# Six blocks of 502 columns instead of eight of 376 in a Fourier transform followed by two MLPs

## The chip, the cores and the metric

One core of a Trainium2 chip runs the whole kernel. The metric is device time in microseconds, the median of several executions of the same program. The tables of cosines and sines are constants of the program, and the inputs lie in device memory when the clock starts.

## The reference

The input `x` has 2 batches of 3008 rows of 256 numbers. A Fourier transform over rows and columns is taken, of which the real part is kept, and every one of the 6016 rows of the result then goes through two MLPs of width 2048:

```python
X = np.fft.fft(x, axis=1)                 # x: 2 x 3008 x 256
X = np.fft.fft(X, axis=2).real
x = X.reshape(6016, 256)
h = x @ moe_w_in                          # 256 -> 2048
x = np.maximum(h, 0.0) ** 2 @ moe_w_out   # 2048 -> 256
h = x @ moe2_w_in
return (h - np.tanh(h)) @ moe2_w_out
```

## The kernel before

**Numbers in two parts.** Every operand of a TensorE product is split into a high part (12 bits) and a low rest, both stored as float32r, and a product is three matmuls: high by high, low by high, high by low (`products`, L350). ScalarE (ACT) makes the high part with a copy, VectorE (DVE) or GpSimd (POOL) the low part with a subtraction.

**The row transform as matmuls.** The rows of the spectrum come in pairs k and -k that share cosine and sine sums, so half of the spectrum is calculated, and each matmul column stands for a pair. There are four classes of k per batch (`KS`), of 378, 376, 376 and 376 columns. Classes 2 and 3 (odd k) come out of one pass, `dft_pair` (48 matmuls, in four PSUM banks); classes 0 and 1 (even k) each out of `dft_mm` (27 matmuls, three banks) on rows that were folded once more (`fold`, the steps from L320 on, then `split_even`). `fold` and `split_even` of the even rows run on POOL for batch 0. The column transform over 256 is multiplied into the first weights instead (`transform_in`).

**Blocks and steps.** A block is one class of one batch: eight blocks of 376 or 378 columns, in the order of `BLOCKS`. The first MLP runs over steps (block, f), f being one of 16 groups of 128 hidden units: `front` makes the hidden units of two halves (6 matmuls, into two of the rotating PSUM banks `w`), `mid` adds and squares them (3 DVE instructions, 3 ACT instructions), `late` makes the low part `gl` (2 POOL instructions), and `back` multiplies by the second weights and adds to four PSUM banks `a` (12 matmuls). `front` runs two steps ahead of `back`. The order of the steps is written out in `STEPS`: the first four f of block 0, all of block 1, the rest of block 0, then block by block.

**What is put beside the steps.** The weights of the first MLP are unpacked from 64-bit integers and transformed while the first steps run; `MADE` says in which step of the loop at L838 which f is made: `transform_in` (4 matmuls with 128 columns, which the profile shows as 8 records), `split_transformed_hi` and `_lo` (L251, L256), and a two-column copy over DMA (`middle_load`, tile `mcol`) after which POOL clears a row (`clear_middle`, L260) and stores two sums (`middle_add`, L274); only then may `front` read that f. The transform is written into the columns from 384 on of the same banks in which `front` put its 376 columns. Then come the folding of the even rows (`bg0`, `bg0s`), loading and folding batch 1 (`bg1`, `bg2`) and preparing the weights of the second MLP (`make_w2`, `bg3`, two pieces a step from step 48 on).

**The second MLP** goes over pairs of f with seven products instead of eight (`pair`, 21 matmuls into three of the `w` banks; `back_pair`, 24 matmuls into the banks `a`), on sums of weights (`sums`) that are loaded once and stay in SBUF for all blocks.

The engines' queues run in order; a scheduler of the tile framework, which sees the written order and the waits, fixes the order in each queue.

Of the kernel before, what the change touches and what calls it, by code (L numbers as in the profile page):

```python
# [9 lines left out]
F32 = mybir.dt.float32  # L10
# [34 lines left out]
BLOCKS = [(b, c) for b in range(B) for c in (2, 3, 0, 1)]  # L45
NBLK = len(BLOCKS)
OFF = np.concatenate([[0], np.cumsum([2 * NC[c] for _, c in BLOCKS])])
NTOT = int(OFF[-1])
# [75 lines left out]
def columns():  # L124
    idx = np.zeros(B * S, np.int64)
    for j, (b, c) in enumerate(BLOCKS):
        k = KS[c]
        for i, kk in enumerate(k):
            if c == 0 and i == NROW:
                continue  # L130
            p, m = int(kk) % S, int(-kk) % S
            if c >= 2 and kk % 4 == 3:
                p, m = m, p
            idx[b * S + p] = OFF[j] + i
            idx[b * S + m] = OFF[j] + NC[c] + i
    return idx


@with_exitstack
def spectral_mlps(  # L140
# [13 lines left out]
    NM = max(NC)  # L154
# [3 lines left out]
    wstack = ctx.enter_context(ExitStack())  # L158
    psw_pool = wstack.enter_context(tc.tile_pool(name="psw", bufs=2, space=PSUM))
# [4 lines left out]
    pools = {}  # L164

    def psw():

        if "w" in pools:
            return [pools["w"].tile([128, 512], F32, tag="w", name=f"w{m}", bufs=4) for m in range(2)]
        t = psw_pool.tile([128, 2, 512], F32, tag="w", name="w", bufs=2)  # L170
        return t

    def bank(p, m):
        return p[m] if isinstance(p, list) else p[:, m]
# [4 lines left out]
    def ring(name):  # L179

        return main.tile([128, 4, NM], F32R, tag="ring", name=name, bufs=8)

    def stage():
        return main.tile([128, 1024], F32, tag="stage", name="stage", bufs=4)
# [7 lines left out]
    wtab = main.tile([128, 2, 2, 128], F32, name="wtab")  # L192
# [48 lines left out]
    def transform_in(f, p):  # L241


        v = val[1, f]
        for m in range(2):
            for kt in range(2):
                cs = slice(kt * 128, (kt + 1) * 128)
                pe.matmul(p[:, m, 384:], wtab[:, kt, m, :], v[:, cs], start=(kt == 0), stop=(kt == 1))

    def split_transformed_hi(f, p):  # L250
        act.copy(wt[f][:, 0, :].rearrange("p (m f) -> p m f", m=2), p[:, :, 384:])  # L251

    def split_transformed_lo(f, p):
        hi = f32(wt[f][:, 0, :]).rearrange("p (m f) -> p m f", m=2)
        dst = wt[f][:, 1, :].rearrange("p (m f) -> p m f", m=2)
        dve.tensor_tensor(dst, p[:, :, 384:], hi, ALU.subtract)  # L256
# [21 lines left out]
    xp = {}  # L278

    def load_x(b, t):  # L280
        r = stage()
        sp.dma_start(r, x[b, t, 0])
        if b == 0:
            u = xp[t] = f32(ring("p")).rearrange("p a n -> p (a n)")[:, :1024]
            sp.dma_start(u, x[b, t, 1])
            for eng, cs in ((dve, slice(640)), (pool, slice(640, 1024))):
                eng.tensor_tensor(r[:, cs], r[:, cs], u[:, cs], ALU.add)
# [4 lines left out]
    def fold(b, t):  # L292

        r = xraw.pop((b, t))
        o = main.tile([128, 2, 4, 128], F32R, tag=f"xs{t}", name=f"xo{t}")
# [22 lines left out]
        e = main.tile([128, 4, 128], F32, tag=f"xf{t}", name=f"xf{t}")  # L318
# [14 lines left out]
    def split_even(b, t):  # L333

        e = main.tile([128, 2, 4, 128], F32R, tag=f"xs{t}", name=f"xe{t}")
# [644 lines left out]
```

## Time and profile before

| | |
|---|---|
| time, median of three executions | 992.44 us (990.68 to 993.64) |
| profiled execution: span from the first to the last instruction | 988.1 us |
| of it, TensorE matmul busy | 956.5 us (97%) |
| VectorE / ScalarE / GpSimd busy | 777.3 / 743.0 / 288.7 us |
| granted TensorE clock | 1.000 |

The page gives the profiled execution's own time as its span; the device time measured around the program adds what lies before the first and after the last instruction. Against the median the span is 4.3 us shorter. PE are matmuls and PEld the weight loads ahead of each of them; matmuls are pipelined, so that two overlap in a busy sum, and the pace is read from starts, not from the mean duration of one.

### The profile page before, as it was taken

The numbers are of one execution on the slowest core, as the hardware profiler recorded it, in microseconds if no ns is written. First come the engines' busy times: TensorE is split into PE (matmuls) and PEld (weight loads), VectorE is DVE, ScalarE is ACT, GpSimd is POOL, SyncE is SP. The second block draws the span as 40 slices with busy tenths as digits, with TensorE's granted clock in tenths as the row PEclk, the third lists the DMA queues.
The fourth block names the chain that finished last, engine by engine and source line by source line (L and its number), as shares of the span: only waits on it lengthen the run. The fifth ranks groups of instructions, "written<-read, shape, count | busy, mean of one in ns | idle before, by whom it ended". The sixth has DMA issues, their size and how long they took to land.

```text
span 988.1 us, 15509 instructions
## 1 busy us (share of the span) xinstructions
PE 956.5 (97%) x5530; PEld 944.8 (96%) x5530; DVE 777.3 (79%) x1444; ACT 743.0 (75%) x1319; POOL 288.7 (29%) x312
## 2 busy tenths in 40 slices
PE   4889999999999999999999999999999999999998
PEld 3778899999999999999899999999999999999998
DVE  5998567878988588888877878778787787877776
ACT  2988868888999789888866767667676676766665
POOL 2276717765676466766500000000000000000000
PEclk9999999999999999999999999999999999999999
DMA  8767031207333343346600101001010010000000
GB/s 313 222 219 187 4 124 29 47 34 242 117 116 131 124 150 120 116 169 230 212 17 1 63 1 64 1 1 64 1 59 5 1 64 1 24 8 1 32 1 32
DMA packets 36334, 82.68 MB, mean 84 GB/s; under 512 B 7328, under 2 KB 21152, under 8 KB 36256
## 3 DMA queue, kind: packets, MB, share of 16 engines
q1 hardware_dynamic: 35280, 79.34, 23.3%
q0 software_dynamic: 976, 2.34, 1.5%
q8 instruction: 43, 0.70, 0.3%
q14 instruction: 35, 0.29, 0.1%
HBM read 55.97 MB, written 25.69 MB: 83 GB/s over the span
## 4 chain that ended last, share of the span: by engine, by line
PE 84%; DVE 7%; ACT 5%; issue 2%; DMA 1%; POOL 1%; SPq 0%; POOLq 0%; DVEq 0%; ACTq 0%
PE w L354 33%; PE a L354 30%; PE a L523 21%; ACT gh L501 1%; DVE pb L492 1%; DVE h L493 1%; DMA p<-x 1%; ACT h L500 1%; DVE h L494 1%; DVE stage L230 1%; ACT h L502 1%; DVE wt L239 1%; DVE val L232 1%; POOL gl L512 1%; ACT val L222 0%
## 5 line engine op out<-in xcount | busy, mean ns | idle before, releaser
L512 POOL TENSOR_TENSOR gl<-h,gh 128x376 fp32r<-128x376 f32 (+1 forms) x240 | 255.3, 1087 | 149.8 <-ACT h L502 109.5
L354 PE MATMUL a<-gh,wt 128*128 128x376 f32 (+1 forms) x1024 | 259.9, 335 | 0.0
L523 PE MATMUL a<-gh,wt 128*128 128x376 f32 (+1 forms) x1024 | 199.9, 336 | 1.7 <-ACT gh L501 1.6
L354 PEld LDWEIGHTS a<-gh,wt 128*128 128x128 f32 x1024 | 184.6, 188 | 0.0
L523 PEld LDWEIGHTS a<-gh,wt 128*128 128x128 f32 x1024 | 178.2, 189 | 4.7 <-ACT gh L501 3.7
L354 PE MATMUL a<-gl,wt 128*128 128x376 f32 (+1 forms) x512 | 171.6, 335 | 0.0
L354 PE MATMUL w<-x,sums 128*128 128x376 f32 (+1 forms) x768 | 163.5, 334 | 1.9 <-ACT m L689 1.9
L354 PE MATMUL w<-uv,wt 128*128 128x376 f32 (+1 forms) x771 | 156.4, 337 | 7.0 <-DVE wt L256 5.1
L680 DVE TENSOR_TENSOR gl<-h,gh 128x376 fp32r<-128x376 f32 (+1 forms) x256 | 138.9, 547 | 11.2 <-ACT gh L678 10.6
L354 PEld LDWEIGHTS w<-uv,wt 128*128 128x128 f32 x771 | 133.9, 188 | 10.0 <-POOL wt L260 3.1
L674 ACT ACTIVATE tanh<-h 128x376 f32<-128x376 f32 (+1 forms) x192 | 99.3, 519 | 56.8 <-DVE h L670 52.0
L678 ACT CAST gh<-h 128x376 fp32r<-128x376 f32 (+1 forms) x256 | 129.3, 507 | 16.5 <-DVE h L676 15.6
L354 PEld LDWEIGHTS w<-x,sums 128*128 128x128 f32 x768 | 135.2, 188 | 2.4 <-ACT m L689 2.2
L676 DVE TENSOR_TENSOR h<-h,tanh 128x376 f32<-128x376 f32 (+1 forms) x192 | 105.2, 549 | 39.9 <-ACT tanh L674 34.7
L500 ACT ACTIVATE h<-h 128x752 f32<-128x752 f32 (+1 forms) x127 | 105.4, 830 | 33.4 <-DVE h L494 29.8
L523 PE MATMUL a<-gl,wt 128*128 128x376 f32 (+1 forms) x512 | 109.5, 336 | 1.2 <-DVE gl L512 0.6
L501 ACT ACTIVATE gh<-h 128x752 fp32r<-128x752 f32 (+1 forms) x128 | 106.8, 834 | 3.1
L502 ACT ACTIVATE h<-h 128x752 f32<-128x752 f32 (+1 forms) x128 | 106.7, 834 | 2.8
L492 DVE SCALAR_TENSOR_TENSOR pb<-ub,w,w 128x376 f32<-128x376 f32 (+1 forms) x127 | 76.3, 600 | 39.0 <-PE w L354 32.3
L670 DVE TENSOR_TENSOR h<-u,w 128x376 f32<-128x376 f32 (+1 forms) x128 | 69.5, 543 | 38.7 <-ACT u L708 38.6
L354 PEld LDWEIGHTS a<-gl,wt 128*128 128x128 f32 x512 | 96.5, 188 | 0.4 <-DVE gl L680 0.3
L523 PEld LDWEIGHTS a<-gl,wt 128*128 128x128 f32 x512 | 90.0, 189 | 2.9 <-POOL gl L512 1.8
(104 smaller groups left out, 1097.3 us busy)
## 6 DMA issues: line engine op xcount, KB each, us to landing
stage<-w SPq DMA_DIRECT2D x32, 512.0 KB, 3.6
tab<-tab SPq DMA_DIRECT2D x12, 752.0 KB, 7.1
w2s<-w SPq DMA_DIRECT2D x16, 512.0 KB, 2.6
wt<-w2s SPq DMA_DIRECT2D x16, 512.0 KB, 3.6
sums<-sums SPq DMA_DIRECT2D x15, 512.0 KB, 3.7
tab<-tab SPq DMA_DIRECT2D x6, 756.0 KB, 6.2
x<-y SPq DMA_DIRECT2D x12, 376.0 KB, 2.8
x2f<-x SPq DMA_DIRECT2D x6, 752.0 KB, 4.7
```

What stands on the lines that cost most here:

```text
L354: pe.matmul(dst, a, r, start=(first and i == 0), stop=(last and i == 3 * len(terms) - 1), **kw)
L492: dve.scalar_tensor_tensor(pb[:, :n], ub[:, :n], w128[:, f:f + 1], bank(p, 0)[:, :n], ALU.mult, ALU.add)
L500: act.activation(h[:, :, :n], h[:, :, :n], AF.Relu)
L501: act.activation(gh[:, :, :n], h[:, :, :n], AF.Square)
L502: last_act[0] = act.activation(h[:, :, :n], h[:, :, :n], AF.Square)
L512: eng.tensor_tensor(gl[:, s, :n], h[:, s, :n], f32(gh[:, s, :n]), ALU.subtract)
L523: pe.matmul(acc[1, blk][m][s][:, :n], wt[f][:, wi, m * 128:(m + 1) * 128], g[:, s, :n], start=first and k == 0, stop=last and k == len(par ...
L670: dve.tensor_tensor(h, c, d, ALU.add)
L674: act.activation(th, c, AF.Tanh)
L676: dve.tensor_tensor(h, c, th, ALU.subtract)
L678: act.copy(gh, h)
L680: dve.tensor_tensor(gl, h, f32(gh), ALU.subtract)
```

## The change

The 1506 columns of a batch are cut into three blocks of 502 columns whatever their class (1506 = 3 x 502), so a block can hold parts of two classes: block 0 has 376 columns of class 2 and 126 of class 3, block 1 has 250 of class 3 and 252 of class 0, block 2 has 126 of class 0 and 376 of class 1. `pieces` lists where the columns of a class go. A step now has matmuls of 502 columns, and there are 96 steps instead of 128; a PSUM bank has room for 512, so the transform of the weights gets a `w` bank of its own.

The first stretch has six f of block 0 (`HALF = 6`) instead of four, then block 1, then the rest. The row transforms of the even classes, and of the odd classes of batch 1, no longer take the banks `a` between two blocks; they go into the rotating `w` banks between steps, one bank's worth (9 matmuls) or two banks' worth (24) at a time, as `DFT` lists. Class 0 of batch 0 is needed by block 1 and is calculated at steps 2 and 3, where it stood at step 20 before; its table is loaded and the even rows folded correspondingly earlier. The 12 matmul pairs of `dft_pair` that use 64 rows each are interleaved so that neighbours use different halves of the rows. `make_w2` advances by three pieces a step instead of two.

SBUF is handed over in stages: a pool `early` for all that belongs to the first MLP's preparation, closed at step 82 and replaced by `later0`; a pool `uvs` for the transformed rows, replaced by `later1` after the last step. The `sums` of the second MLP have four buffers and are loaded again for every block, three pairs ahead.

```diff
+NB = 502
+PER = sum(NC) // NB
+NBLK = B * PER
-HALF = 4
-DFT = {(0, HALF): (2, 3), (3, 0): (4,), (5, 0): (6, 7)}
+HALF = 6
+W2_DONE = 82
...
+TABS = {-2: (0, 0), 4: (0, 1), 20: (1, 2), 44: (1, 0), 58: (1, 1)}
+DFT = {2: [(0, 0)], 3: [(0, 0), (0, 0)], 16: [(0, 1)], 17: [(0, 1)], 18: [(0, 1)], 39: [(1, 2)], 42: [(1, 2)]}
+DFT |= {52 + k: [(1, 0)] for k in range(3)} | {68 + k: [(1, 1)] for k in range(3)}
...
+def pieces(b, c):
+    at = 0
+    while at < NC[c]:
+        blk, to = divmod(START[c] + at, NB)
+        n = min(NC[c] - at, NB - to)
+        yield b * PER + blk, slice(to, to + n), slice(at, at + n)
+        at += n
...
-            return [pools["w"].tile([128, 512], F32, tag="w", name=f"w{m}", bufs=4) for m in range(2)]
-        t = psw_pool.tile([128, 2, 512], F32, tag="w", name="w", bufs=2)
+    def wbank():
+        return ps.tile([128, 512], F32, tag="w", name="w", bufs=4)
...
-                pe.matmul(p[:, m, 384:], wtab[:, kt, m, :], v[:, cs], start=(kt == 0), stop=(kt == 1))
+                pe.matmul(p[:, m * 128:(m + 1) * 128], wtab[:, kt, m, :], v[:, cs], start=(kt == 0), stop=(kt == 1))
...
+    def uv_of(blk):
+        if blk not in uv:
+            uvt = uvs.tile([128, 2, 2, NB], F32R, tag="uv", name="uv", bufs=3)
+            ub = main.tile([128, NB], F32, tag="ub", name="ub", bufs=3)
...
+    def put(piece, m, src):
+        blk, to, at = piece
+        uvt = uv_of(blk)[0]
+        act.copy(uvt[:, m, 0, to], src[:, at])
+        dve.tensor_tensor(uvt[:, m, 1, to], src[:, at], f32(uvt[:, m, 0, to]), ALU.subtract)
...
+    def dft_single(b, c):
...
+        for slot, i, m in ((3 - 2 * c, 0, None), (3 - 2 * c, 1, 1), (2 * c, 0, 0)):
+            p = wbank()
+            products(p[:, :n], [term(slot, i, t, m is None) for t in range(3)])
+            for piece in pieces(b, c):
+                if m is None:
+                    put_special(piece, p)
+                else:
+                    put(piece, m, p)
+            yield
...
-        eng = dve if blk == 0 and f < NF // 2 else pool
+        eng = dve if blk == 0 and f < HALF else pool
...
+    def load_sums(n):
+        if n < NBLK * (NF // 2):
+            u = later[0].tile([128, 2, 512], F32R, tag="sums", name="sums", bufs=4)
+            sp.dma_start(f32(u).rearrange("p h n -> p (h n)"), sums_d[n % (NF // 2)])
...
-        s1, s2, s3, s4 = sums[j]
+        s1, s2, s3, s4 = sums.pop(blk * (NF // 2) + j)
+        load_sums(blk * (NF // 2) + j + 3)
...
     for i in range(-2, NS - 2):
         blk, f = STEPS[i] if i >= 0 else (0, i)
-        if i == max(MADE) + 2:
-            wstack.close()
+        for key in DFT.get(i, ()):
+            if key not in dfts:
+                if key[1] == 0:
+                    step(splits[key[0]])
+                dfts[key] = pair_blocks(key[0]) if key[1] == 2 else dft_single(*key)
+            step(dfts[key], 1)
         look(i + 2)
         if i in MADE:
-            p = wps[STEPS[i + 2]]
...
+            p = wbank()
             transform_in(w, p)
...
-        if 1 <= i < NF + HALF:
-            with tc.issue_after(begun.ins):
-                step(bg0, 2)
...
+        if i < 2:
+            with tc.issue_after(begun[0].ins):
+                step(bg0, 3)
+        elif i >= NF and not any(ends(*STEPS[k]) for k in (i, i + 1)):
...
+                    step(bg3, 3)
+        if i == W2_DONE:
+            step(bg3)
+            later[0] = open_pool("later0", "left")
+            for n in range(3):
+                load_sums(n)
```

How it moves instructions shows in two queues. The first is POOL's near the start of the program, before the change: after the three additions of the loaded rows (L287) come the clearings and sums for the weights f = 0 to 3 (`wt_0` to `wt_3`), and the folding of the even rows (L321, L323, of the tile `p`; L325, of `xf`) stands behind them.

```order
L287 TENSOR_TENSOR stage<-stage,p 128x384 x3
L274 TENSOR_TENSOR w_69<-mcol 128x1
L260 MEMSET wt_0_233 1x2x128
L260 MEMSET wt_1_271 1x2x128
L260 MEMSET wt_2_309 1x2x128
L260 MEMSET wt_3_343 1x2x128
L321 TENSOR_TENSOR p<-p 128x256
L323 TENSOR_TENSOR p<-p 128x256
L260 MEMSET wt_4_383 1x2x128
L325 TENSOR_TENSOR xf_476<-p 128x256
```

The same queue with the change (line numbers are those of the changed kernel; `xp` is what `p` was, `xe_527` the split even rows of the first third, L271 the clearing):

```order
L300 TENSOR_TENSOR stage<-stage,xp 128x384 x3
L334 TENSOR_TENSOR xp<-xp 128x256
L336 TENSOR_TENSOR xp<-xp 128x256
L338 TENSOR_TENSOR xf_355<-xp 128x256
L271 MEMSET wt_0_233 1x2x128
L271 MEMSET wt_1_278 1x2x128
L271 MEMSET wt_2_320 1x2x128
L341 TENSOR_TENSOR xf_355<-xp 128x128
L352 TENSOR_TENSOR xe_527<-xf_355,xe_527 128x512
L271 MEMSET wt_3_368 1x2x128
L352 TENSOR_TENSOR xe_530<-xf_405,xe_530 128x512
L271 MEMSET wt_4_416 1x2x128
```

Folding now starts ahead of the first clearing, and the folds of all three thirds stand between the clearings for f = 2 and f = 5; the last third (`xe_533`) follows the clearing for f = 4.

The second queue is PE's. Before the change the row transform of class 0 (tile `xe`, tables `tab`) stands at step 20, behind the end of block 1, in banks `a`, and the next step's `front` (L354 with `uv`) follows all of it:

```order
L354 MATMUL a_1321<-tab_1118,xe_1033 128x378 x3
L354 MATMUL a_1321<-tab_1120,xe_1116 128x378 x3
L354 MATMUL a_1321<-tab_1122,xe_1194 128x378 x3
L354 MATMUL a_1320<-tab_1118,xe_1033 128x378 x3
L354 MATMUL a_1359<-tab_1261,xe_1033 128x376 x3
L354 MATMUL w_1395<-uv,wt_7_540 128x376 x3
```

With the change the first third of it stands in the middle of block 0's third step, around the `front` of f = 4 (`wt_4`) and inside the `back` of f = 2 (L535):

```order
L261 MATMUL w<-val,wtab 128x128 x4
L368 MATMUL w<-tab_336,xe_527 128x378 x3
L368 MATMUL w<-tab_338,xe_530 128x378 x3
L368 MATMUL w<-uv,wt_4_416 128x502 x3
L535 MATMUL a_417<-gh,wt_2_320 128x502
L368 MATMUL w<-uv,wt_4_416 128x502 x3
L535 MATMUL a_419<-gh,wt_2_320 128x502
L535 MATMUL a_418<-gh,wt_2_320 128x502
L368 MATMUL w<-tab_340,xe_533 128x378
L535 MATMUL a_420<-gh,wt_2_320 128x502
```

So PE's queue, which runs in order, reaches the matmuls on `xe_527`, `xe_530` and `xe_533` in the fifth pass of the loop instead of the twenty-third, and `front` and `back` of block 0 stand behind them.

## Rows read from the trace of the kernel before

**Rows 1.** The page, engines: busy time, share of the span, instructions.

```profile
PE 956.5 (97%) x5530; PEld 944.8 (96%) x5530; DVE 777.3 (79%) x1444; ACT 743.0 (75%) x1319; POOL 288.7 (29%) x312
```

**Rows 2.** Windows: from:to, length, then busy time (instructions) of each engine.

```profile
20.00:120.00 100.00, 87.78 (x522) 81.00 (x519) 84.69 (x149) 84.88 (x144) 59.31 (x91) 1.00 0.57 165
120.00:480.00 360.00, 359.71 (x2082) 357.45 (x2081) 291.11 (x502) 306.64 (x420) 219.88 (x206) 1.00 0.37 127
560.00:920.00 360.00, 360.00 (x2087) 359.92 (x2087) 280.72 (x562) 248.85 (x541) 0.00 (x0) 1.00 0.06 20
```

**Rows 3.** Groups of PE, 20 to 120 us: count, busy us, mean ns, idle before, releasers.

```profile
L354 PE MATMUL w<-uv,wt 128*128 128x376 f32 x135 | 29.6, 348 | 7.0 <-DVE wt L256 5.1 <-POOL wt L260 1.8
L248 PE MATMUL w<-val,wtab 128*128 128x128 f32 x128 | 18.3, 276 | 1.9 <-DVE val L232 1.9
```

**Rows 4.** Timeline of PE at two places: start, us, what, count.

```profile
14.29 2.71 PE L354 MATMUL a<-tab,xo 128*128 128x376 f32 x8
...
16.48 0.52 PE L354 MATMUL a<-tab,xo 128*128 128x376 f32 x1
...
48.06 1.05 PE L248 MATMUL w<-val,wtab 128*128 128x128 f32 x8
```

**Rows 5.** Timeline of PE: the first step's front, a later front.

```profile
28.78 2.02 PE L354 MATMUL w<-uv,wt 128*128 128x376 f32 x9
...
63.99 1.28 PE L354 MATMUL w<-uv,wt 128*128 128x376 f32 x6
```

**Rows 6.** Groups of POOL, 17 to 120 us.

```profile
L512 POOL TENSOR_TENSOR gl<-h,gh 128x376 fp32r<-128x376 f32 x32 | 33.3, 1068 | 5.8 <-ACT h L502 5.8
...
L260 POOL MEMSET wt<- 1x256 f32 x16 | 4.9, 309 | 18.6 <-DMA mcol<-wt 15.8 <-ACT wt L236 2.7
L339 POOL TENSOR_TENSOR xe<-xf,xe 128x512 fp32r<-128x512 f32 x3 | 3.9, 1291 | 0.0
L323 POOL TENSOR_TENSOR p<-p 128x256 f32<-128x256 f32 x3 | 2.9, 974 | 0.2
...
L321 POOL TENSOR_TENSOR p<-p 128x256 f32<-128x256 f32 x3 | 2.6, 881 | 0.0
L325 POOL TENSOR_TENSOR xf<-p 128x256 f32<-128x256 f32 x3 | 2.2, 720 | 0.0
L328 POOL TENSOR_TENSOR xf<-p 128x128 f32<-128x128 f32 x3 | 1.5, 513 | 0.0
L329 POOL TENSOR_TENSOR xf<-p 128x127 f32<-128x127 f32 x3 | 1.3, 447 | 0.0
L330 POOL TENSOR_TENSOR xf<-p 128x1 f32<-128x1 f32 x3 | 1.1, 365 | 0.0
```

**Rows 7.** Timeline of POOL: its first sum after the loads, the clearing for f = 2.

```profile
31.39 0.75 POOL L274 TENSOR_TENSOR w<-mcol 128x1 f32<-128x1 f32 x1 [14.22 <-ACT stage L224]
...
38.39 0.30 POOL L260 MEMSET wt<- 1x256 f32 x1 [4.99 <-DMA mcol<-wt]
```

**Rows 8.** Groups of DVE and ACT, whole span, by shape.

```profile
L680 DVE TENSOR_TENSOR gl<-h,gh 128x376 fp32r<-128x376 f32 x192 | 103.9, 547 | 8.8 <-ACT gh L678 8.2
L230 DVE SCALAR_TENSOR_TENSOR stage<-val,stage 128x512 int32<-128x512 int32 x32 | 31.0, 972 | 0.2
L500 ACT ACTIVATE h<-h 128x752 f32<-128x752 f32 x95 | 78.8, 829 | 26.5 <-DVE h L494 23.0 <-POOL gl L512 1.1 <-POOL xf L325 0.8
```

**Rows 9.** Groups of DVE, first 45 us.

```profile
L230 DVE SCALAR_TENSOR_TENSOR stage<-val,stage 128x512 int32<-128x512 int32 x7 | 4.8, 688 | 0.2
```

**Rows 10.** DMA issues: queue, count, KB each, median us to landing.

```profile
sums<-sums SPq DMA_DIRECT2D x15, 512.0 KB, 3.7
```

**Rows 11.** Timeline where the second MLP begins, and the last matmul and copy.

```profile
484.22 1.30 PE L354 MATMUL w<-x,sums 128*128 128x376 f32 x6 [1.92 <-ACT m L689]
...
983.90 0.33 PE L354 MATMUL a<-gl,wt 128*128 128x376 f32 x1
984.27 0.55 DVE L750 COPY y<-a 128x376 f32<-128x376 f32 x1 [0.58 <-PE a L354]
```

More of the change, by code (lines that the diff above doesn't have):

```diff
@@ new lines, in pair_terms, with dft_pair @@
+    def pair_terms(b, t, m, r):
+        n = NC[2]
+        T, e = tab[b, 2][t], xo[b, t]
+        rows = slice(64 * r, 64 * r + 64) if t == 1 else slice(0, 128)
+        for i in range(2):
+            w = [e[rows, h, 2 * m + (i ^ m)] for h in range(2)]
+            v = [T[rows, 2 * i + h, :n] for h in range(2)]
+            for k, (x, y) in enumerate(((0, 0), (1, 0), (0, 1))):
+                yield w[x], v[y], t == r and i == k == 0, t == r + 1 and i == 1 and k == 2
+    def dft_pair(b, t, m, banks):
+        terms = [list(pair_terms(b, t, m, r)) if t != 2 - 2 * r else [] for r in range(2)]
+        for k in range(6):
+            for r in range(2):
+                if terms[r]:
+                    w, v, first, last = terms[r][k]
+                    pe.matmul(banks[r][:, :NC[2]], w, v, start=first, stop=last)
@@ new lines, in pair_take @@
+    def pair_take(b, m, d, v):
+        n = NC[2]
+        act.copy(v[:, 0, :n], d[1][:, :n])
+        for k, op in ((1, ALU.add), (0, ALU.subtract)):
+            dve.tensor_tensor(v[:, k, :n], d[0][:, :n], v[:, 0, :n], op)
+        yield
+        for blk in range(b * PER, b * PER + 2):
+            for q in range(2):
+                for piece in pieces(b, 2 + q):
+                    if piece[0] != blk:
+                        continue
+                    put(piece, m, v[:, 1 - q])
+                    if m == 1:
+                        _, to, at = piece
+                        for i in range(2):
+                            pe.matmul(d[1 - q][:, at], sel, uv[blk][0][:, 1, i, to], start=(i == 0), stop=(i == 1))
+                        put_special(piece, d[1 - q])
+            yield
@@ L795, in spectral_mlps @@
     conv_parts(1, 2)
-    pe0 = pair_evac(0)
-    step(pe0, 1)
-    n = NC[BLOCKS[0][1]]
-    vneg = main.tile([128, 2, 2, NM], F32R, tag="uv", name="vneg", bufs=2)[:, 0]
+    takes = [pair_take(0, m, first[m], main.tile([128, 2, NB], F32, tag="h", name="dt", bufs=3)) for m in (1, 0)]
+    for _ in range(2):
+        for g in takes:
+            step(g, 1)
+    vneg = uvs.tile([128, 2, 2, NB], F32R, tag="uv", name="vneg", bufs=3)[:, 0]
     for i in range(2):
-        act.activation(vneg[:, i, :n], f32(uv[0][0][:, 1, i, :n]), AF.Copy, scale=sign)
-    weights1(1, wps[0, 1])
+        act.activation(vneg[:, i], f32(uv[0][0][:, 1, i]), AF.Copy, scale=sign)
+    p = wbank()
+    weights1(1, p)
     middle_load(1)
@@ L805, in spectral_mlps @@
     conv_parts(1, 3)
-    step(pe0)
+    for g in takes:
+        step(g)
     middle_add(0)
@@ L821, in next_batch @@
             yield from fold(1, t)
-    def next_even():
-        for t in range(3):
-            yield from split_even(1, t)
-    bg0, bg0s, bg1, bg2, bg3 = even_rows(), even_splits(), next_batch(), next_even(), make_w2()
+    bg0, bg1, bg3 = even_rows(), next_batch(), make_w2()
+    splits = [even_splits(b) for b in range(B)]
     NS = len(STEPS)
-    TABS = {14: 2, 18: 3, 2 * NF + 2: 4, 4 * NF + 2: 6, 4 * NF + 12: 7}
+    dfts = {}
     fronts = set()
```

313 lines of the change are left out of this document (115 added, 198 removed).

## The prediction

> **What bounds the kernel now.** I read the page's engines first, then the windows, then PE's pace, then the queues that PE waits for at the start. PE is busy for 97% of the span and the next engine, DVE, for 79% [rows 1]. The windows split this: from 120 to 480 us, the first MLP once its weights are ready, PE idles 0.3 us in 360, and from 560 to 920 us, in the second MLP, not at all; from 20 to 120 us it idles 12 us in 100 [rows 2]. So almost everywhere the time is the number of matmuls times their pace, and there is one stretch with waits.
>
> The pace: 2087 matmuls in 360 us are 172.5 ns each [rows 2]. At the granted clock of 1.00, the upper level of 2.4 GHz, 376.5 columns (the mean of the four classes) take 156.9 ns. So each matmul takes 15.6 ns more than its columns. The busy sum hides waits, since two matmuls overlap in it; the same pace gives the true loss of the start. Of 522 records from 20 to 120 us [rows 2] 128 belong to the small matmuls of the weights' transform [rows 3], which follow one another every 0.11 us: eight in 1.05 us, the last of them 0.276 long [rows 3, 4]. That is 394 x 0.1725 + 128 x 0.11 = 82 us of work in 100: 18 us are lost. The waits named are for the low part of transformed weights (`wt` L256, 5.1 us) and for the cleared row (L260, 1.8 us) [rows 3]. Between the first front (28.78 us) and the ninth step's (63.99) a pass takes 4.40 us [rows 5], where PE's own work is 18 x 0.1725 + 8 x 0.11 = 3.99.
>
> **The change part by part.**
>
> *Fewer, longer matmuls.* Both MLPs together have 96 + 192 matmuls per block in the first and 168 + 192 in the second: 648 a block, 5184 in eight blocks and 3888 in six, so 1296 fewer. The columns are the same, 8 x 376.5 = 6 x 502. The span has no matmul of 502 columns, so its price is bounded from both sides. Where the 15.6 ns belong to each matmul, one of 502 takes 209.2 + 15.6 = 224.8 ns, and the change saves 1296 x 15.6 = 20.2 us. Where they are a tenth on every column, it takes 230 ns and saves nothing. Where the weight load, not the columns, sets 172.5, the matmul of 502 could come down to its bare 209.2 ns and the change would save 3888 x 15.6 = 61 us on top of 20: 81.
>
> I take the fixed price. The one other pace at this clock is that of the small matmuls: 128 columns every 110 ns, of a plain f32 product in two records each with 128 columns, so the columns alone can't be read off it; but it shows that a weight load of 128 columns can be had every 110 ns, and a load can't be what sets 172.5. Against a tenth per column speaks the start: eight starts from 14.29 to 16.48 us lie 313 ns apart [rows 4], which is 376 columns at the lower level of 1.2 GHz to the nanosecond, although the profile prints 1.000 as its mean clock. At half the pace the surplus is gone, so it is not a share of the columns that the array needs anyway; it is something of which a slow matmul hides all. A weight load that gets in the way of the moving columns, once a matmul, does that, and its cost would stay one load's. A limit on reading the moving operand would do it too, and that would go with the columns; I can't exclude it.
>
> The Trainium skill, "TensorE: Matmul & The Clock Gate", section "Wait — 56ns, not 53.3ns?", gives start to start as the columns at 2.4 GHz plus about 2.5 ns per matmul. By it the fixed part is small and 1296 matmuls give back 3.2 us. Its 159.4 ns for 376.5 columns don't agree with the 172.5 of the windows, and it says nothing of the other 13 ns.
>
> *The start: the even rows and class 0.* `dft_single` for class 0 stands in the fifth to sixth pass. It needs all three `xe`, which POOL folds. A third of that takes 0.88 + 0.97 + 0.72 + 0.51 + 0.45 + 0.37 + 1.29 = 5.2 us [rows 6], in all 15.6. POOL idles 14.2 us before 31.39 [rows 7], but only 2.6 us of folding are queued there; the remaining 13.0 stand behind the clearing for f = 2, which ends at 38.7 [rows 7], and between the clearings for f = 3 and 4, which wait for copies over DMA (15.8 us in the 16 clearings before [rows 6]). So `xe_533` is ready at 51.7 us at the earliest, with the copies in between at 57, which I take. PE reaches it after 63 matmuls of 502, 6 of 378 and four transforms, 14.2 + 1.0 + 3.5 = 18.7 us from the first front: at 47.5. Behind the waiting matmul stand the rest of `back` of f = 2 and all that follows on PE; DVE and ACT wait for those. This is 9.5 us of waiting, where the passes of before lost 35.2 - 8 x 3.99 = 3.3 us up to 63.99 and some more in `front` and `back` of f = 0, 1, which have less work than a pass (8 us by the same counting).
>
> *The start: later passes.* Before, a pass with weights asks DVE for three operations of about 0.55 us and four of the weights, of which the largest two take about 0.97 each with POOL at work [rows 8] and 0.69 without [rows 9]: 4.4 us, the pass's length, against 3.99 of PE. With 502 columns an operation takes 0.68 (547 ns for 376 and 688 for 512 columns [rows 8, 9], so 1.04 ns a column); DVE then needs 2.0 + 2.75 = 4.8 us in a pass with weights, PE 18 x 0.225 + 0.88 = 4.9, and only nine of the fourteen passes from i = 3 on have any. So of the 18 us about 4 before the first front stay, 9.5 come in the class 0 passes, and 2 to 3 remain later: 16. I count 2 us gained; with `xe_533` at 52 or at 65 us it is 7 gained or 6 lost.
>
> *Small terms.* Interleaving the 64-row pairs lets twelve of them run two abreast, where today part of them does: -0.7 us, between 0 and -2. The transform's own `w` bank makes three banks a pass of four, so a front's second bank is free when DVE has read the first bank of the front one pass earlier, and 4.9 us of PE work lie in between; DVE needs that one operation at the head of a pass, so 0. `make_w2` at three pieces in 4.05 us instead of two in 3.1 us is 15% denser; between 120 and 480 us DVE is at 81% and ACT at 85% [rows 2], so it fits, with +1 us for the passes that get `put` and splits too (0 to 4). POOL's two `gl` grow from 1.07 [rows 6] to about 1.4 us, 2.9 in 4.05. ACT's three instructions of 1004 columns come to some 1.05 us each from 829 ns for 752 [rows 8], 3.1 in 4.05. The 48 loads of `sums` take 3.7 us each [rows 10] and are issued three pairs (30 us) ahead with the DMA engines at 6% [rows 2]: 0. That work is the cover; without it each load would cost up to 3.7. The handover at step 82 waits on preparation that is done some six steps earlier: 0. The gap of 1.9 us where the second MLP begins [rows 11] comes from DVE and ACT work that grows like the steps: 0, with 2 either way. The tail from the last matmul at 983.90 [rows 11] has a copy and a DMA a third wider: +0.3.
>
> **Sum.** 988.1 - 20.2 - 2 - 0.7 + 1 + 0.3 = 966.5 us of span. The median of the runs lies 4.3 us above the span that was profiled, and that stays: 970.8, which I round to 970.
>
> **The rivals.**
>
> *The surplus goes with the columns* (17%). Then the first term is 0 and the time is 991. For it: nothing in the trace separates 376 from 378 columns well enough. Against: the paragraph on the pace. The page's rule cited above comes out close by, at 988 (3.2 us of the 20.2); its chance is inside this one.
>
> *Half of it* (8%): 980. Both mechanisms may add.
>
> *Loads set the pace* (3%): 3888 x 15.6 us more, 910. Against it stands the 110 ns of the small matmuls.
>
> *DVE becomes the bound while `make_w2` runs* (7%), which ends on the other side. About 35 steps carry three pieces. With its largest operations at 0.97 us [rows 8] a piece is some 0.64 us; DVE needs 2.0 + 1.9 = 3.9 us of a step's 4.05. Every 0.1 us above 4.05 costs 3.5 us, since the hidden units of the next step queue behind the pieces. From 4.7 us a step on, 23 us, the kernel is slower than before; at 4.9 it ends at 1000. For it: POOL's longer `gl` run beside them, and 0.97 instead of 0.69 us is what DVE's operations take where POOL works [rows 8, 9]. Against: the 0.97 is already in the 3.9.
>
> **How the numbers follow.** The likeliest case, 65%, gives 970, by itself 962 to 979 with the bounds of the start and the small terms. The range 958 to 991 holds nearly all of it, the half case, half of the columns case and the first part of DVE's: about 8 in 10. A measurement of this kernel tells apart about 0.3%, 3 us. Faster takes 64 of the likeliest case's 65, the half and the loads case, and a quarter of the columns case: 0.80. Same is half of the columns case and a little of the others: 0.10. Slower, the rest of it and DVE's: 0.10.
>
> **What would show it.** The windows of the second MLP: 225 ns a matmul (about 1600 in 360 us) if the surplus is fixed, 230 (1565) if it goes with the columns, 209 (1720) if loads set it. From 20 to 120 us: waits for `xe` before the class 0 matmuls at about 47 to 57 us, and hardly any for L267, the low part of transformed weights, after 70 us. From 210 to 370 us: PE without gaps and DVE below 95%. The prediction is wrong if the pace is 230 or more, or if PE idles over 10 us anywhere behind the first 120.

## The result and the profile after

The changed kernel takes 982.03 us (median of 4 runs, 981.34 to 984.63), beside 992.11 for the kernel before in the same comparison: a ratio of 0.9911, 95% interval 0.989 to 0.9932. It is faster, and inside the range, but by 10 us where 22 were forecast. A second measurement (`after_again` below) gave 983.3, 8.5 below the kernel before, and a profile with a span of 980.8. The execution profiled below took 984.63 us (span 982.9, 5.2 below the span before). Here, as in every run on record, the time is 1.8 us above the span; so of the 4.3 us between the median and the span of the kernel before about 2.5 come from a profiled execution that was faster than the median, and the one profiled here is slower than its median. Marks of the two profiles show 5 of the 10 us.

The page's engines and three windows of the changed kernel (columns as in [rows 1, 2]):

```profile
PE 952.6 (97%) x4238; PEld 786.5 (80%) x4238; DVE 762.5 (78%) x1152; ACT 697.2 (71%) x1043; POOL 278.8 (28%) x252
```

```profile
20.00:120.00 100.00, 90.20 (x432) 75.49 (x429) 85.95 (x139) 81.43 (x135) 46.67 (x65) 0.93 0.45 146
120.00:480.00 360.00, 356.42 (x1593) 293.57 (x1592) 289.72 (x416) 293.55 (x342) 220.46 (x173) 1.00 0.37 126
...
560.00:920.00 360.00, 360.00 (x1581) 297.24 (x1580) 273.53 (x425) 232.08 (x411) 0.00 (x0) 1.00 0.22 75
```

Against [rows 2]: in the second MLP PE is still without a gap, and 1581 matmuls in 360 us are 227.7 ns each, not 224.8. The first MLP, whose pace is read in experiment 6, has gaps now (3.6 us in 360, before 0.3), and the start runs at a granted clock of 0.93. Marks from PE's timeline (start, us, what, count, idle before) cut the span into three:

```profile
23.30 0.99 PE L430 MATMUL a<-tab,xo 128*128 128x376 f32 x2 [2.95 <-ACT xo L327]
...
33.36 3.67 PE L368 MATMUL w<-uv,wt 128*128 128x502 f32 x9 [0.67 <-ACT uv L383]
...
483.58 1.53 PE L368 MATMUL w<-x,sums 128*128 128x502 f32 x6
...
978.63 0.38 PE L368 MATMUL a<-gl,wt 128*128 128x502 f32 x1
```

Beside [rows 5, 11]: the first front starts 4.6 us later (33.36 for 28.78), the first MLP is 5.2 us shorter (450.2 for 455.4), the second 4.6 (495.05 for 499.68). The forecast had 11.2 for the second MLP alone (2880 x 172.5 - 2160 x 224.8 ns).

**Where the start loses.** POOL and DVE at the folds of the third part of x, from their timelines:

```profile
17.39 1.35 DVE L300 TENSOR_TENSOR stage<-stage,xp 128x640 f32<-128x640 f32 x1
18.85 1.03 DVE L316 TENSOR_TENSOR xp<-stage 128x512 f32<-128x512 f32 x1
19.80 1.22 DVE L318 TENSOR_TENSOR xp<-stage 128x512 f32<-128x512 f32 x1
...
16.88 1.19 POOL L334 TENSOR_TENSOR xp<-xp 128x256 f32<-128x256 f32 x1
18.14 1.19 POOL L336 TENSOR_TENSOR xp<-xp 128x256 f32<-128x256 f32 x1
```

In this kernel POOL begins the even rows' folds here, as soon as its part of L300 is done, and DVE's three operations take 3.6 us; with POOL idle the same three take 0.81 + 0.69 + 0.68 = 2.2 (the kernel `late_folds` below). The third `xo` comes that much later, PE idles 2.95 us for it, and from 22.7 us on the clock is at its lower level for a time, and again from 32.9: nine matmuls of 502 columns at 33.36 take 3.67 us, where the same nine take 2.29 at the upper level (in the kernel `padded_rows` below).

**Where the first MLP loses.** DVE, ACT and PE around 336 us, from their timelines:

```profile
331.46 1.73 DVE L597 TENSOR_TENSOR w<-val,w 128x512 fp32r<-128x512 f32 x1
333.12 1.36 DVE L605 TENSOR_TENSOR sums<-val 128x128 f32<-128x128 f32 x1
334.40 0.28 DVE L606 TENSOR_TENSOR sums<-val 128x128 f32<-128x128 f32 x1
...
334.77 0.67 ACT L235 ACTIVATE val<-stage 128x512 f32<-128x512 f32 x1 [2.09 <-DVE sums L606]
335.34 1.03 ACT L513 ACTIVATE gh<-h 128x1004 fp32r<-128x1004 f32 x1
...
336.42 2.09 PE L535 MATMUL a<-gh,wt 128*128 128x502 f32 x8 [0.70 <-ACT gh L513]
```

These are pieces of `make_w2`, two of them slow beside POOL's `gl`, which runs from 331.4 to 334.3 us (1.73 and 1.36 us; operations of the same sizes take 0.69 and 0.28 without it). ACT's own piece waits for DVE, and the squares of the next hidden units (L513) stand behind it in ACT's queue; PE waits for them.

### The profile page after: what moved, and what is told of

Its sections match the earlier page's. It is cut to its first block, busy times and chain, and to the rows that moved or that the text cites. A ratio compares the mean times of both kernels' runs of the same rounds, so it can differ in the third digit from the quotient of the medians.

```text
span 982.9 us, 12126 instructions
## 1 busy us (share of the span) xinstructions
PE 952.6 (97%) x4238; PEld 786.5 (80%) x4238; DVE 762.5 (78%) x1152; ACT 697.2 (71%) x1043; POOL 278.8 (28%) x252
## 4 chain that ended last, share of the span: by engine, by line
PE 90%; DVE 3%; issue 2%; POOL 2%; ACT 2%; DMA 1%; SPq 0%; DVEq 0%; POOLq 0%; ACTq 0%
PE w L368 37%; PE a L368 27%; PE a L535 24%; DMA xp<-x 1%; PE w L261 1%; POOL gl L524 1%; PE w L430 1%; ACT gh L513 1%; PE a L430 0%; DVE h L506 0%; DVE h L505 0%; DVE pb L504 0%; DVE sums L605 0%; ACT h L514 0%; DVE y L569 0%
## 5 line engine op out<-in xcount | busy, mean ns | idle before, releaser
L524 POOL TENSOR_TENSOR gl<-h,gh 128x502 fp32r<-128x502 f32 x180 | 243.4, 1376 | 157.3 <-ACT h L514 137.1
L368 PE MATMUL a<-gh,wt 128*128 128x502 f32 x768 | 237.5, 390 | 0.0
L535 PE MATMUL a<-gh,wt 128*128 128x502 f32 x768 | 194.7, 395 | 5.2 <-ACT gh L513 5.0
L535 PEld LDWEIGHTS a<-gh,wt 128*128 128x128 f32 x768 | 145.1, 190 | 39.0 <-ACT gh L513 7.9
L686 ACT CAST gh<-h 128x502 fp32r<-128x502 f32 x192 | 117.1, 612 | 64.0 <-DVE h L684 63.5
L688 DVE TENSOR_TENSOR gl<-h,gh 128x502 fp32r<-128x502 f32 x192 | 130.4, 679 | 39.6 <-ACT gh L686 35.4
L368 PE MATMUL w<-x,sums 128*128 128x502 f32 x576 | 154.3, 389 | 0.0
L368 PE MATMUL w<-uv,wt 128*128 128x502 f32 x579 | 151.5, 396 | 1.0 <-ACT uv L383 0.7
L368 PE MATMUL a<-gl,wt 128*128 128x502 f32 x384 | 149.8, 390 | 0.0
L512 ACT ACTIVATE h<-h 128x1004 f32<-128x1004 f32 x95 | 98.8, 1040 | 36.5 <-DVE h L506 36.3
L684 DVE TENSOR_TENSOR h<-h,tanh 128x502 f32<-128x502 f32 x144 | 97.7, 679 | 32.3 <-ACT tanh L682 29.0
L535 PE MATMUL a<-gl,wt 128*128 128x502 f32 x384 | 103.7, 393 | 0.6 <-POOL gl L524 0.5
L513 ACT ACTIVATE gh<-h 128x1004 fp32r<-128x1004 f32 x96 | 100.3, 1045 | 1.8
L514 ACT ACTIVATE h<-h 128x1004 f32<-128x1004 f32 x96 | 100.1, 1043 | 1.9
L504 DVE SCALAR_TENSOR_TENSOR pb<-ub,w,w 128x502 f32<-128x502 f32 x95 | 69.4, 731 | 26.7 <-PE w L368 26.2
L535 PEld LDWEIGHTS a<-gl,wt 128*128 128x128 f32 x384 | 72.2, 189 | 17.2 <-POOL gl L524 1.7
```

Of the source, the lines that this page charges most:

```text
L368: pe.matmul(dst, a, r, start=(first and i == 0), stop=(last and i == 3 * len(terms) - 1), **kw)
L504: dve.scalar_tensor_tensor(pb[:, :n], ub[:, :n], w128[:, f:f + 1], p[0][:, :n], ALU.mult, ALU.add)
L512: act.activation(h[:, :, :n], h[:, :, :n], AF.Relu)
L513: act.activation(gh[:, :, :n], h[:, :, :n], AF.Square)
L514: last_act[0] = act.activation(h[:, :, :n], h[:, :, :n], AF.Square)
L524: eng.tensor_tensor(gl[:, s, :n], h[:, s, :n], f32(gh[:, s, :n]), ALU.subtract)
```

## The experiments

Three questions: what sets the pace of a matmul, what the start lost, and what the gaps in the first MLP cost. Kernels that hold matmuls alone compute nothing of the reference; the edits of the others leave the computation whole.

**1. The pace by width** (`pace_by_width`): 64 matmuls a line, moving rows from one tile, eight weights in turn.

> A kernel of matmuls alone: series of 64 matmuls on the same operands, each series with another width (128 to 512 columns), another start of the moving operand (0, 2, 8, 16 elements), one stationary operand or eight, one PSUM bank or four, float32r or bf16. It leaves the whole computation out and writes zeros. The two kernels' traces have 172.4 ns at 376 columns and 228.1 at 502. Theory 'mostly on the columns': a straight line through both, 5.8 ns + 0.443 ns a column: 116 ns at 250, 148 at 320, 201 at 440, 233 at 512, the same wherever the operand starts. Theory 'fixed 15.6 ns, and the 502 columns of the changed kernel pay 3.3 ns for where their rows start (2008 bytes apart)': at start 0 the widths 250, 440, 502, 512 take 120, 199, 224.8, 229 ns, and 502 takes 228 at starts of 2 or 8 elements only. Theory 'in steps of so many columns': 376 and 378 differ by over 1.5 ns, 502 and 504 not at all. bf16 at 376 and 502: 159 and 212 ns if the surplus is that of reading four bytes a column.

PE's timeline (start, us, count); a pace is the distance of two starts by 64:

```profile
47.96 11.25 PE L186 MATMUL bank<-mv,wts 128*128 128x376 f32 x64
59.05 11.26 PE L187 MATMUL bank<-mv,wts 128*128 128x378 f32 x64
70.14 11.26 PE L188 MATMUL bank<-mv,wts 128*128 128x384 f32 x64
81.24 12.96 PE L189 MATMUL bank<-mv,wts 128*128 128x440 f32 x64
...
108.33 14.46 PE L191 MATMUL bank<-mv,wts 128*128 128x502 f32 x64
122.62 14.67 PE L192 MATMUL bank<-mv,wts 128*128 128x504 f32 x64
137.13 14.69 PE L193 MATMUL bank<-mv,wts 128*128 128x512 f32 x64
151.66 11.26 PE L194 MATMUL bank<-mv,wts 128*128 128x376 f32 x64
...
199.07 14.75 PE L198 MATMUL bank<-mv,wts 128*128 128x502 f32 x64
213.65 14.68 PE L199 MATMUL bank<-mv,wts 128*128 128x502 f32 x64
228.17 14.47 PE L200 MATMUL bank<-mv,wts 128*128 128x502 f32 x64
...
256.77 10.36 PE L202 MATMUL bank<-mb,wtb 128*128 128x376 bf16 x64
266.97 13.71 PE L203 MATMUL bank<-mb,wtb 128*128 128x502 bf16 x64
```

376, 378 and 384 columns take the same 173.3 to 173.4 ns; 502 take 223.3, 504 and 512 take 226.7 and 227.0. It is neither a straight line nor a share of the columns, and the surplus over the columns at 2.4 GHz is no larger at 502 (14.1 ns) than at 376 (16.6): the bare test comes near the forecast's 224.8, and the changed kernel's 227.7 does not. With the rows 32 bytes further (L198) the same 502 columns take 227.8. The Trainium skill, "TensorE: Matmul & The Clock Gate", section "Wait — 56ns, not 53.3ns?", which the prediction weighed with its 2.5 ns a matmul, holds here for bfloat16: 376 columns in 159.4 ns, 156.7 + 2.7. It does not hold for the float32r of this kernel.

**2. The start, folds later** (`late_folds`, with `after_again`, the changed kernel once more).

```diff
-                begun[0] = eng.tensor_tensor(r[:, cs], r[:, cs], u[:, cs], ALU.add)
+                eng.tensor_tensor(r[:, cs], r[:, cs], u[:, cs], ALU.add)
...
-    middle_add(0)
+    begun[0] = middle_add(0)
```

> The folding of the even rows may start on POOL only behind the sum for the first weights, as in the kernel before. Theory 'POOL's early folds slow DVE's last folds of the odd rows': DVE's L318 of the last third falls from 1.22 to 0.7 us, PE's wait for the third xo from 2.95 us to 1.2 to 1.5, the first front starts at 29 to 30.5 us instead of 33.4, TensorE's clock does not fall at 23 us; the even rows are ready 2.5 to 3 us later, so 2 to 3 us come back as waits for xe; total 1 to 4 us faster than the changed kernel. Rival 'the first front is late by the three extra special columns and the larger splits, not by POOL': it still starts at 33 us and the time is the same or 2 us worse.

> The changed kernel unaltered, for the same chip as the others: 980 to 984 us.

983.09 us against 983.3. PE's and DVE's timelines in `late_folds`:

```profile
19.51 0.68 DVE L318 TENSOR_TENSOR xp<-stage 128x512 f32<-128x512 f32 x1
...
22.48 0.61 PE L430 MATMUL a<-tab,xo 128*128 128x376 f32 x2 [1.43 <-ACT xo L327]
...
30.42 3.83 PE L368 MATMUL w<-uv,wt 128*128 128x502 f32 x9 [0.68 <-ACT uv L383]
```

The place was right: DVE is back at 0.68 us, the wait for the third `xo` at 1.43, the first front 2.9 us earlier than in the profile above and 2.0 earlier than in that of `after_again`. The time did not follow. The last third of the even rows is split at 58.65 us here and at 58.76 in `after_again`, so what was won in front of it is lost again by then; and the clock still falls, now between 30 and 48 us (granted 0.92 from 32 to 66; 1.00 in `after_again`).

**3. The gaps of the first MLP** (`spread_w2`).

```diff
-                elif i < 38:
-                    step(bg1, 2)
+                elif i < 34:
+                    step(bg1, 2 + i % 2)
                 else:
+                    step(bg1)
...
-                    step(bg3, 3)
+                    step(bg3, 2 + i % 2)
```

> Preparation of the second weights at two and three pieces a step in turn from step 34 on instead of three from step 38 on (batch 1's folds at two and three a step until 33). Theory 'three pieces a step overrun DVE and ACT in places': PE's losses between 200 and 480 us, 8.4 us in the changed kernel, fall to 3 to 5, total 3 to 5 us faster. Rival 'those losses come from the row transforms in the w banks and from block ends': losses stay within 1.5 us of 8.4 and the time is the same.

986.55 us (ratio 0.9955, 0.9941 to 0.9969): slower than the changed kernel by 3 us, which neither theory had. The gaps around 336 us are nearly gone (PE waits 0.8 us for `gh` from 200 to 480), and one wait in front of the second batch's class 2 transform, at 237 us, takes their place (us in total, times, longest):

```profile
PE w L448 <- ACT uv L383: 3.6, 1, 3.6
```

Behind this wait the granted clock is 0.50 from 240.8 to 244.2 us; in the changed kernel's profile it is 1.00 from 120 to 480. At half the clock these 3.4 us cost about 1.7 (an estimate), so that one long wait costs more than itself.

**4. Class 0 a step later** (`class0_later`): `DFT = {3: [(0, 0)], 4: [(0, 0), (0, 0)], ...` for `{2: ..., 3: ...`.

> The changed kernel with the class 0 transform of the first batch one step later (steps 3 and 4 for 2 and 3). Theory lateness (TensorE waits for xe at 54 to 62 us, 3.2 us in five pieces, because the even rows' folds and splits are late): 1 to 3 us faster than the changed kernel, 980 to 982 us. Rival, the same work is late next (with the early folds moved, what was won at 20 us was lost again by 66 us): 982 to 984 us, the waits then in front of other matmuls of the first 66 us.

984.95 us, 2 us slower than the changed kernel, so nearer the rival. The waits for `xe` are gone from the list of 14 to 120 us. Of the 3.2 us that were expected there the changed kernel's list puts 1.0 on `xe`; PE now waits longer for the hidden units of other steps (4.4 us for 2.7).

**5. Order, company, rows** (`pace_by_order`, `padded_rows`). In the second, `gh`, `gl`, `uv`, `b11` and `x2` keep 502 columns in rows of 512:

```diff
-        gh = main.tile([128, 2, NB], F32R, tag="gh", name="gh", bufs=3)
+        gh = main.tile([128, 2, PITCH], F32R, tag="gh", name="gh", bufs=3)
```

> Matmuls alone again, this time in the kernel's own orders (two rows by two banks under one pair of weights, as in the first MLP; three into one bank, as in the second), with row pitches of 502, 504 and 512 elements, and then with VectorE, ScalarE and GpSimd at work beside them. In the changed kernel one of 502 columns takes 228.1 ns from start to start, in the first bare test 223.3. Theory rows (where the rows lie sets it): about 228 at a pitch of 502, 223.5 at a pitch of 512, quiet or not. Theory neighbours (other engines' reads and writes cost it): 223 to 224 at either pitch while it is quiet, about 228 with the engines busy. Theory order (a new row, bank and weights with each matmul): about 228 at every pitch, quiet too. At 376 columns each theory has 172 to 174, as before the change.

> The changed kernel with its moving rows (uv, gh, gl, b11, x2) at a pitch of 512 elements, still 502 columns a matmul. Theory rows: the pace falls from 228 to 224 ns or less, 3888 matmuls make 12 to 18 us, so 965 to 971 us. Theories neighbours and order: the pace stays at 228 and the time at 981 to 984 us.

PE's timeline of `pace_by_order`: L202 and L204 quiet, L211 and L213 with the other engines at work, at pitches of 502 (L202, L211) and 512:

```profile
50.58 21.77 PE L202 MATMUL bank<-g,wts 128*128 128x502 f32 x96
72.18 22.23 PE L203 MATMUL bank<-g,wts 128*128 128x502 f32 x96
94.25 21.62 PE L204 MATMUL bank<-g,wts 128*128 128x502 f32 x96
115.71 21.98 PE L205 MATMUL bank<-g,wts 128*128 128x504 f32 x96
...
219.08 21.78 PE L211 MATMUL bank<-g,wts 128*128 128x502 f32 x96
240.70 0.39 PE L189 MATMUL gate<-mv,wts 128*128 128x502 f32 x1
240.93 21.61 PE L213 MATMUL bank<-g,wts 128*128 128x502 f32 x96
262.37 0.34 PE L189 MATMUL gate<-mv,wts 128*128 128x376 f32 x1
```

225.0 and 223.5 ns quiet, 225.2 and 223.3 busy: company costs nothing, and neither does the order. A pitch of 504 (L203) takes 229.9. So where the rows lie moves the pace by 6 ns, yet in the second MLP the padded kernel stays at its old pace, 228.3 (x1577):

```profile
560.00:920.00 360.00, 360.00 (x1577) 297.91 (x1576) 271.94 (x425) 230.59 (x410) 0.00 (x0) 1.00 0.21 75
```

All three theories in their plain form fall. The padded kernel takes 978.94 us (ratio 0.9892, 0.9874 to 0.991), and it wins these 3 to 4 us outside the second MLP, in part by the pace of the first (next experiment).

**6. Rows and weights together** (`pace_by_place`, then `weights_moved` and `aligned`). The weights have places too: 13 of the 16 tiles of `wt` start 96 bytes past a multiple of 128. `weights_moved` widens small tiles so that all start at a multiple of 128; `aligned` does that and pads the rows, so that rows also start there.

```diff
-    sign = main.tile([128, 1], F32, name="sign")
+    sign = main.tile([128, 16], F32, name="sign")[:, :1]
...
-        mcol[f] = main.tile([128, 2], F32, tag="mcol", name="mcol", bufs=2)
+        mcol[f] = main.tile([128, 16], F32, tag="mcol", name="mcol", bufs=2)
...
-            ub = main.tile([128, NB], F32, tag="ub", name="ub", bufs=3)
+            ub = main.tile([128, PITCH], F32, tag="ub", name="ub", bufs=3)
```

> Matmuls alone, in the order of twelve steps of the first MLP and at the very addresses that uv, gh, gl and the weights have in the changed kernel; then with the weights moved by 32 bytes, with the rows at a pitch of 512, with both, and with rows and weights moved so that both start 96 bytes past a multiple of 128. The padded kernel showed that a pitch of 512 alone wins 3 to 4 us and leaves the pace at 227.7 ns. Theory place (where rows and weights lie against each other): the first sequence shows the kernel's 228 ns, and at least one of the moved ones 224 or less, which is then worth up to 15 us in the kernel. Theory company (something of the running kernel that bare matmuls don't have): the first sequence shows 223 to 225 as in both bare tests, and the others differ from it by some 2 ns either way. At 376 columns 170 to 173.

> The changed kernel with some small tiles widened, so that every weight tile starts at a multiple of 128 bytes (before: 96 bytes past one, for 13 of 16); the moving rows keep their pitch of 502 elements. Theory place: the bare test won 1.5 ns a matmul by it (229.3 to 227.8), so 3888 matmuls make 4 to 8 us: 975 to 979 us, the pace at 226 to 227 ns. Rival, company (the running kernel's pace doesn't hang on places): 982 to 984 us, the pace at 228.

> As weights_moved, and all moving rows of the two MLPs at a pitch of 512 elements and starting at multiples of 128 bytes. Theory place: in the padded kernel the matmuls whose row, and the next one's weights, start at such multiples took 225.1 ns, so 3888 by 2 to 3 ns make 8 to 12 us: 971 to 976 us. If the bare sequence's best (227.1) is all there is to get: 977 to 979, as padded_rows. Company: 979 to 984 us.

PE's timeline of `pace_by_place`, the first row of each sequence of 216 matmuls:

```profile
44.10 1.54 PE L202 MATMUL bank<-U,WT 128*128 128x502 f32 x6
...
93.63 1.55 PE L203 MATMUL bank<-U,WT 128*128 128x502 f32 x6
...
142.83 1.60 PE L204 MATMUL bank<-U,WT 128*128 128x502 f32 x6
...
192.41 1.53 PE L205 MATMUL bank<-U,WT 128*128 128x502 f32 x6
...
241.48 1.53 PE L206 MATMUL bank<-U,WT 128*128 128x502 f32 x6
...
290.53 1.19 PE L207 MATMUL bank<-U,WT 128*128 128x376 f32 x6
```

At the addresses of the changed kernel's first MLP bare matmuls take 229.3 ns (49.53 us by 216): nothing else of the kernel is needed for its slow pace. Moved weights (L203) give 227.8, padded rows (L204) 229.5. The last two sequences (L205, L206), 227.2 and 227.1, have rows and weights at equal places only in part: in L205 `uv` lies 64 bytes off, and in L206 `uv` and the weights start 96 bytes past a multiple of 128, but `gh` and `gl` 32, not 96 as the expectation says.

In the kernels the first MLP answers too. Two fronts of PE's timeline with the same 234 matmuls of 502 columns and no gap between them, in the changed kernel and then in `padded_rows`:

```profile
142.53 1.54 PE L368 MATMUL w<-uv,wt 128*128 128x502 f32 x6
...
196.13 1.54 PE L368 MATMUL w<-uv,wt 128*128 128x502 f32 x6
```

```profile
139.66 1.51 PE L369 MATMUL w<-uv,wt 128*128 128x502 f32 x6
...
193.01 1.52 PE L369 MATMUL w<-uv,wt 128*128 128x502 f32 x6
```

That is 229.1 and 228.0 ns; the same stretch gives 227.4 in `weights_moved` and 223.5 in `aligned`. The first MLP, from first front to the start of the second, takes 443.6 us in `padded_rows` and 443.7 in `weights_moved`, for 450.2: 2 to 3 of these 6.6 us are the pace (1728 matmuls), about 1 shorter gaps, the rest was not traced. The two kernels' second MLP (first `weights_moved`, then `aligned`):

```profile
560.00:920.00 360.00, 360.00 (x1579) 297.06 (x1578) 272.26 (x425) 231.20 (x410) 0.00 (x0) 1.00 0.22 75
```

```profile
560.00:920.00 360.00, 360.00 (x1612) 302.14 (x1611) 277.59 (x434) 236.44 (x419) 0.00 (x0) 1.00 0.22 76
```

In the second MLP weights alone leave the pace at 228.0, rows alone at 228.3, both give 223.3. The times: `weights_moved` 978.31 us (ratio 0.9876, 0.9853 to 0.9899), `aligned` 973.45 (0.9818, 0.9798 to 0.9839). Where each row and weight starts in the programs' memory allocation, in bytes past a multiple of 128, with the pace at 502 columns:

| matmuls | rows | weights | ns |
|---|---|---|---|
| one row (L191 of experiment 1) | 32 | 32 | 223.3 |
| one row, 8 bytes on (L197) | 40 | 32 | 223.8 |
| one row, 32 bytes on (L198) | 64 | 32 | 227.8 |
| one row, 64 bytes on (L199) | 96 | 32 | 226.9 |
| two rows, pitch 512 (L204 of experiment 5) | 96, 96 | 96 | 223.5 |
| two rows, pitch 502 (L202) | 96, 56 | 96 | 225.0 |
| two rows, pitch 504 (L203) | 32, 0 | 96 | 229.9 |
| `aligned`, second MLP | 0 | 0 | 223.3 |

The pace of 223.3 to 223.5 appears where all rows and weights start at one and the same place, at each of the three places tried (0, 32 and 96). Why, no run here shows.

**7. The old width at good places** (`before_aligned`): the kernel before, rows of 376 at a pitch of 384, `sign` and `mcol` widened in the same way, so that every row and weight starts at a multiple of 128 bytes.

```diff
-    NM = max(NC)
+    NM = 384
```

> The kernel before the change, with every weight tile and every moving row at a multiple of 128 bytes (rows of 376 columns at a pitch of 384). It tells what the place is worth at the old width. If a good place wins at 376 columns as it does at 502 (4 to 5 ns of 228): 172.4 to 168 to 170 ns, 5184 matmuls make 12 to 20 us, 972 to 980 us, and the wider blocks are worth nothing beside it. If the place matters little at 376 (bare runs gave 170.1 to 173.4 ns there, and 173.4 for 384 columns): 172 to 173.5 ns, 985 to 995 us, and at equal places the wider blocks win what the forecast had said.

993.05 us (ratio 1.0023, 1.001 to 1.0035), and 172.9 ns a matmul in the second MLP, where [rows 2] gave 172.5:

```profile
560.00:920.00 360.00, 360.00 (x2082) 359.98 (x2081) 278.96 (x557) 248.31 (x538) 0.00 (x0) 1.00 0.06 20
```

At 376 columns equal places win nothing. At equal places the wider blocks win 993.05 - 973.45 = 19.6 us. That this is near the forecast's 20.2 is chance: the paces alone would give 5184 x 172.9 - 3888 x 223.4 = 28 us, of which some 8 are lost again (experiment 8).

**8. What is lost again** (`aligned_late`, `aligned_spread`): `aligned` with the edit of `late_folds`, and then with `make_w2` started three steps earlier and two pieces for three in ten steps.

```diff
-                    step(bg3, 3)
+                    step(bg1)
+                    step(bg3, 2 if i in LIGHT else 3)
```

> As aligned, and the even rows' folds on GpSimd begin only behind the first middle row, as in late_folds, where that moved the losses of the first 66 us and won nothing. Expected: within 1 us of aligned; if the better start counts for itself, 1 to 2 us faster.

> As aligned_late, and make_w2 starts three steps earlier and takes two pieces instead of three in steps 38 to 43, 60, 61, 76 and 77, where TensorE waits for gh behind VectorE's pieces in aligned_late (7 of 12 us lost between 190 and 425 us). Theory pieces: 2 to 4 us faster than aligned_late, 968 to 970 us. Rival, they are only moved to the class 2 transform, as in spread_w2: 971 to 974 us.

`aligned_late` takes 971.92 us (ratio 0.9807, 0.9787 to 0.9827), the lowest median here, with an interval that overlaps that of `aligned`; `aligned_spread` 975.04 (0.9837, 0.9819 to 0.9855), so its theory failed. From the changed kernel to `aligned` the second MLP gets 9.0 us shorter (486.0 for 495.05), the first only 0.9 (449.3 for 450.2), although its pace fell by 5.6 ns. The window of `aligned`, and PE's longest waits in it:

```profile
120.00:480.00 360.00, 349.85 (x1595) 291.85 (x1594) 297.19 (x417) 294.34 (x343) 222.45 (x173) 1.00 0.37 126
```

```profile
PE a L536 <- ACT gh L514: 5.8, 5, 1.6
```

PE now idles 10.2 us in that window, where the changed kernel had 3.6: the 1595 matmuls are as many as before (1593). There PE waits for what DVE and ACT do for the second batch and `make_w2` beside the steps, although neither is busy for more than 83% of the window (297.19 of 360). Spreading the pieces only moved the waits (`aligned_spread` idles 11.5 us there), for the second time, and again the clock fell: 0.50 from 225.6 to 229.0 and from 334.8 to 338.2 us, at waits of 1.7 and 2.4 us, where `aligned_late` has 1.00 in the whole window.

## Why the prediction was wrong, and where it was right

**The bound** was read rightly: nearly all of the span is matmuls times pace, before and after.

**The pace term failed, in size.** The step reads "one of 502 takes 209.2 + 15.6 = 224.8 ns, and the change saves 1296 x 15.6 = 20.2 us". Measured are 229.1 ns in the first MLP and 227.7 in the second, so that it is 5184 x 172.5 - 1728 x 229.1 - 2160 x 227.7 = 6.5 us. These 13.7 us are the miss: 970 + 13.7 is 984, and 982 and 983 were measured. The mechanism, a cost per matmul that does not grow with the columns, was right: at equal places the surplus is 16.0 ns at 376 columns (172.9 - 156.9) and 14.1 at 502. That the weight load causes it, as the prediction supposed, no run shows. What the step left out is that the surplus hangs on where the operands lie in SBUF. At 502 columns it is 14 ns at equal places and 18.5 to 20 at the changed kernel's, whose rows of 2008 bytes each start elsewhere than the last and than the weights. In the old kernel it is 16 ns with unequal and with equal places, so the trace of before could not show it. The rival in which half of the surplus goes with the columns gave 980, close to the time and for another reason: what it takes for a share of the columns goes away with `aligned`. The forecast's own signs of being wrong, a pace of 230 or 10 us of idle time, did not appear: they were set too wide for a miss of half the gain.

**The start** was forecast to win 2 us. In the profiled execution the first front comes 4.6 us late (3.7 in `after_again`, at 32.4 us), which the forecast did not have: POOL's folds slow DVE's beside them. The 9.5 us of waiting for `xe` were too much: the list of waits shows 1.0 (2.0 in `after_again`), and an experiment that took them away was slower. By the forecast's own way of counting, with 229.1 ns for 502 columns, 20 to 120 us lose 18 us in this profile and 15 in `after_again`, where it had 16. That it comes so near is luck, two errors that cancel.

**`make_w2`** was given +1, bounds 0 to 4; the first MLP's window idles 3.3 us more. The mechanism was that of the slower rival, hidden units queued behind pieces. Its price of 0.97 us for a large operation "where POOL works" was misread: that is the mean of all 32, of which half take about 0.69 us and the others 1.0 to 2.1 (in the changed kernel 21 take about 0.69 and 11 take 1.2 to 1.8). So the sum of a step can fit (3.9 of 4.05 us) and a slow pair of pieces still holds up the queue. At 229.1 ns a matmul this costs 3 us, at 223.5 it costs 10.

**The small terms** held: no wait where the second MLP begins (1.9 us before), no wait for `sums`, a tail of the same length.

Open: why equal places are fast at 502 columns and not at 376; why half of the cure helps the first MLP and not the second; and what makes the clock fall in the first 66 us, since two executions of the changed kernel with nearly the same waits were granted 0.90 and 1.00 from 32 to 66 us.

## What to carry to other kernels

When a change alters the width of matmuls, the pace of the old width does not give that of the new one: measure it bare, a few microseconds of matmuls at the new width and at the addresses the kernel will use, rows and weights. Then give rows a padded pitch and let rows and weights start at the same place modulo 128 bytes; here that nearly doubled what the change won; by halves it won 1 to 2 ns a matmul in the first MLP and nothing in the second, and at the old width it won nothing. And when the bounding engine gets faster, look for the stretch in which others have less slack: of the 19 us that the better pace promised (1728 x 5.6 + 2160 x 4.4 ns) 9 stayed there.

## What the runs showed of the hardware

- float32r matmuls at the upper clock level, rows and weights 32 bytes past a multiple of 128: 173.3 ns at 376, 378 and 384 columns alike, 223.3 at 502 and 227.0 at 512; 376 columns of bfloat16 take 159.4.
- The pace of 502 columns runs from 223.3 to 229.9 ns with the starts of rows and weights alone, with all other engines idle; other engines at work change it by 0.2 ns or less. At 376 columns it runs from 170.1 (`pace_by_order`, L201, unequal places) to 173.3, so equal places are no gain there.
- DVE operations beside POOL's: 0.68 us became 1.22 (L318), 0.69 became 1.73 (L597). The Trainium skill, "SBUF — State Buffer", section "SBUF: two separate sides", has the two engines share a port pair of which one holds all for a whole instruction; these rows agree in that both operations, with two inputs in SBUF, get slower, but not all do: L504, with an input in PSUM, keeps 0.73 us beside POOL's `gl` (at 329.42 us).
